# A bilinear-GLU transformer block: the order of work ahead of the first Strassen block

## The chip, the cores and the metric

The kernel runs on one core of one Trainium2 chip, in fp32. The metric is the device time of one execution in microseconds. The core has TensorE (PE, with its weight loads PEld), VectorE (DVE), ScalarE (ACT), GpSimd (POOL) and a queue for DMAs on SyncE (SP). Each engine takes its instructions in the order in which the program issues them.

## What is computed

The input x is 2048 tokens by 512. From c come six vectors: shifts, scales and gates of two adaptive layer norms.

```
h = layernorm(x) * (1 + ca) + sa
x = x + ga * (linear attention of h, 32 heads of 16) @ wo
h = layernorm(x) * (1 + cb) + sb
x = x + gb * (((h @ w_gate) * (h @ w_up)) @ w_down)      # F = 1376
```

## The kernel before

The tokens are handled in four chunks (0 to 3) of four tiles of 128. Products are made in three matmuls from a rounded high part and a low part of each operand: a split is a copy on ScalarE (L196, high part) and a subtraction (L197, low part) on VectorE or GpSimd. The schedule is manual: the order of the calls is the order on every engine.

Tiles 8 to 15 of the attention queries are flipped by VectorE: `move_in` brings a tile in block order from DRAM, `turn_v(i)` (L722) transposes its 32x32 blocks on VectorE, `turn_h(i)` (L676) makes the high part on ScalarE and `turn_l(i)` (L680) the low part on VectorE. `y_seed(i)` (L746) writes the residual into a PSUM bank on ScalarE, `y_a(i)` (L755) adds 12 matmuls to it, and `y_b(i)` copies the sum back (L763, ScalarE) and takes its layer-norm statistics (L229, VectorE). Tiles 12 to 15 alternate between two PSUM banks, so a seed waits for the statistics of the tile two before. `y_step(i)` calls `y_a(i)`, then, if the next tile has been turned but not split, its `turn_h` and `turn_l`.

The second feed-forward product pairs chunks (0, 1) and later (2, 3) in a Strassen scheme over tiles of 128 columns of F (1376 columns make ten tiles and one of 96). Columns 8 to 10 are done in the plain way for chunks 0 and 1 (`gate_up`, `down`), and `down(1, (2, 3))` is the last such call: its matmuls go out at once, and it returns a function that evacuates its two tiles, added to x, on VectorE (L824).

A Strassen block has a left and a right side. The left, `first`, is two objects `Left` (k = 0, 1); each has sums s1 to s4, and `split` makes their high and low parts on ScalarE and VectorE. The right, `rights[n]`, has four differences of 128x256 each, made by `right_sums(n, on)` (L994), and `right_split(n)`: first four high parts on ScalarE (`high`: L1005 for b11, L1008 for t1 and t2 together, t3 and t4, b21 and b22), then four low parts on GpSimd (`lows`, L1012), in that order.

`ffn()` is a generator of blocks; `fill(n)` runs n of its steps. Each block has seven products of six matmuls (`times`, L1026) in four PSUM banks a, b, c, d, in this order, with the copies on ScalarE (`copy`, L1031) between them:

```
times(a, A["a11"], R["b11"], True)
copy(b, a)
times(d, A["s1"], R["t1"], True)
copy(p5, d)
times(b, A["s2"], R["t2"], False)      # adds to the copy of a
copy(c, b); copy(u2, b)
times(a, A["a12"], R["b21"], False)
times(c, A["s3"], R["t3"], False)      # L1085 adds p5 on VectorE
times(d, A["s4"], R["b22"], False)     # L1089, L1054
times(c, A["a22"], R["t4"], False)
```

Within one product the six matmuls go by k = 0, 1, and for each k: high right with high left, high right with low left, low right with high left. At the third product VectorE also scales the down weights (L1171), and at the fifth the next block's `right_split` is issued.

In the kernel before, one `fill(1)` follows `y_step(14)`, which issues `turn_h(15)` and `turn_l(15)` behind `y_a(14)`; `turn_v(15)` stands last of VectorE's work ahead of it, behind `right_sums(0)`, the evacuations of `down(1, (2, 3))` and the low parts of s1 and s2 for k = 1.

Of the kernel before, what the change touches and what calls it, by code (L numbers as in the profile page):

```python
# [24 lines left out]
def tile_adaln_block(  # L25
# [12 lines left out]
    nc = tc.nc  # L38
# [31 lines left out]
    def f32(ap):  # L70
        return ap.bitcast(F32)
# [7 lines left out]
    def B(tag, shape=(P, D), dt=F32):  # L79

        return T(tiles, tag, shape, dt)

    def acc_bank():
        return T(ps_acc, "acc")

    def bank():
        return T(ps_w, "bank")
# [216 lines left out]
    def proj(i, w, of=bank):  # L304

        ch, j = divmod(i, NJ)
        ps = of()
        product(ps, [(cut(norm[ch].t[k], j * P, (j + 1) * P), w[k]) for k in range(KD)])
        return ps
# [43 lines left out]
    def q_a(i, ps):  # L353
        phq[i] = B("h")
        q_ps[i] = ps
        phi_a(ps, phq[i])
# [311 lines left out]
    def turn_a(i):  # L668
        tps[i] = turn_bank[0]()
        phi = phq.pop(i)  # L670
        for k in range(KD):
            nc.tensor.transpose(tps[i][:, k * P:(k + 1) * P], phi[:, k * P:(k + 1) * P], ident)

    def turn_h(i):
        pqs[i] = (B("xh", dt=F32R), B("xl", dt=F32R))
        nc.scalar.activation(pqs[i][0], tps[i], AF.Copy)  # L676

    def turn_l(i):
        h, l = pqs[i]
        nc.vector.tensor_tensor(l, tps.pop(i), f32(h), op=ALU.subtract)  # L680
# [30 lines left out]
    def move_in(*tiles):  # L711

        for i in tiles:
            v = moved[i].rearrange("(m i) (q c) -> q i m c", i=BL, c=P)
            moved[i] = B("u")
            for q in range(NQ):
                nc.sync.dma_start(moved[i][q * BL:(q + 1) * BL].rearrange("i (m c) -> i m c", c=P), v[q])

    def turn_v(i):

        tps[i] = B("f")
        nc.vector.transpose(tps[i].rearrange("p (s m i) -> p m s i", m=NQ, i=BL),  # L722
                            moved.pop(i).rearrange("p (m i s) -> p m s i", m=NQ, i=BL))

    def turned_v(i):
        turn_v(i)
        turn_h(i)
        turn_l(i)

    def ready(*tiles):  # L730
        den_c(*tiles)
        move_out(*tiles)
# [7 lines left out]
    def y_seed(i, of=acc_bank):  # L740

        yps[i] = of()
        if of is bank:

            nc.tensor.matmul(yps[i], wp[0][0][:, :P], wp[0][0], start=True, stop=True)
        nc.scalar.activation(yps[i], xts[i // NJ][i % NJ], AF.Copy)  # L746

    def y_a(i):
        if i not in yps:
            y_seed(i)  # L750
        pq = pqs.pop(i)
        for k in range(KD):
            (ah, al), (bh, bl) = cut(pq, k * P, (k + 1) * P), (wp4 if i in FLIPPED else wp)[k]
            for x, y in ((ah, bh), (ah, bl), (al, bh)):
                nc.tensor.matmul(yps[i], x, y, start=False, stop=k == KD - 1 and x is al, skip_group_check=True)  # L755

    def y_b(i):
        ch, j = divmod(i, NJ)
        ps = yps.pop(i)
        if ch in SUMS:  # L760
            norm2[ch].stats_act(j, ps)
            return
        nc.scalar.activation(xts[ch][j], ps, AF.Copy)  # L763
        norm2[ch].stats(j, of=ps)

    def y_step(i, *more, late=(), q=None, turn=True, seed=acc_bank):

        if q is not None:
            ps = proj(q, wq)
        if turn and i + 1 < NT and i + 1 not in pqs and i + 1 not in FLIPPED:  # L770
            turn_a(i + 1)
        y_a(i)
        if i + 1 in tps:
            turn_h(i + 1)
            turn_l(i + 1)
        if seed is acc_bank and i + 1 < NT:
            y_seed(i + 1, seed)
        if i - 1 in yps:
            y_b(i - 1)
        if q is not None:  # L780
            q_a(q, ps)
        if seed and i + 1 < NT and i + 1 not in yps:
            y_seed(i + 1, seed)
        for do in more:
            do()
        for do in late:
            do()
# [32 lines left out]
    def evac(ch, dn, js=range(NJ), last=False, cols=((0, D),)):  # L820
        for j in js:
            xt = xts[ch][j]
            for a, b in cols:
                nc.vector.tensor_tensor(xt[:, a:b], dn[j][:, a:b], xt[:, a:b], op=ALU.add)  # L824
                if last:
                    nc.sync.dma_start(ov[ch, j, :, a:b], xt[:, a:b])
# [26 lines left out]
    def down(ch, js=range(NJ), ahead={}, parts=(lone,), dn=None):  # L853

        dn = dn or {j: acc_bank() for j in js}
        for step, (part, j) in enumerate((part, j) for part in parts for j in js):
            for do in ahead.get(step, ()):
                do()
            a, b = j * P, (j + 1) * P
            for f in part:  # L860
                n = fts[f][1]
                (hh, hl), (dh, dl) = hs[ch, f], wf[f][2]
                nc.tensor.matmul(dn[j], hh[:n, a:b], dh[:n], start=f == lone[0], stop=False)
                nc.tensor.matmul(dn[j], hh[:n, a:b], dl[:n], start=False, stop=False)
                nc.tensor.matmul(dn[j], hl[:n, a:b], dh[:n], start=False, stop=f == lone[-1])
        return lambda: evac(ch, dn, js)
# [270 lines left out]
    def right_sums(n, on=None):  # L1137
        if n < len(steps):
            rights[n].sums(on)

    def right_split(n, on=None):
        if n < len(steps):
            rights[n].high()
            rights[n].lows(on)
# [3 lines left out]
    def draw_load(n):  # L1148
        if n < len(steps):
            f0, k = fts[steps[n][1]]  # L1150
            draws[n] = load(w_down[f0:f0 + k, :], "raw")

    banks = []
# [45 lines left out]
    def fill(n):  # L1199
        for _ in range(n):  # L1200
            next(work, None)
# [64 lines left out]
    take = down(0, ahead={1: (lambda: move_in(9), lambda: ready(11)),  # L1266
                          3: (lambda: turned_v(8), lambda: y_seed(8, bank), lambda: move_in(10, 11), lambda: turn_v(9))})
# [6 lines left out]
    first = [Left((0, 1), k).into(side) for k in range(KH)]  # L1274
# [36 lines left out]
    take = down(1, (0, 1), parts=((f0, f1), (f2,)), dn=dn, ahead={2: (lambda: y_a(12),)})  # L1311
# [1 line left out]
    take()  # L1313
    y_b(12)
    turn_v(14)
    take = down(1, (2, 3))
    first[1].sum("s1", "s3", "s2", "s4", on=nc.gpsimd)
    y_seed(14, y_bank)
    turn_h(14)
    first[0].split("s1", "s2")  # L1320
    turn_l(14)
    y_b(13)
    y_seed(15, y_bank)
    right_sums(0, nc.vector)
    take()
    first[1].split("s1", "s2")
    turn_v(15)
    for n in range(4):
        banks.append(bank())
    banks[:] = [banks[n] for n in (2, 0, 1, 3)]  # L1330
    turn_bank[0] = acc_bank
    right_split(0)
    draw_load(0)
    stash, second_side, plan = {}, {}, {}
    work = ffn()
    y_step(14, seed=None)
    fill(1)
    y_b(14)
    right_sums(1, nc.vector)
    first[0].split("s3", "s4")  # L1340
    fill(1)
    first[1].split("s3", "s4")
    fill(2)
    y_step(15)
    fill(2)
    y_b(15)
# [68 lines left out]
```

## Time and profile before

| | |
|---|---|
| Median of 3 runs | 558.47 us (558.44 to 559.93) |
| The profiled execution | 559.39 us in all, span 557.7 us |
| TensorE busy | 550.1 us, 99% of the span |
| VectorE busy | 377.8 us, 68% |
| ScalarE busy | 291.4 us, 52% |
| GpSimd busy | 203.0 us, 36% |
| Granted TensorE clock, mean | 0.997 |

A row of the timeline reads: start from the span's start, duration (of all the instructions that the row merges), engine, line, operation, output and inputs, form, count, and in brackets the idle time before it with what ended it. The start is that of dispatch; an instruction that then has to wait for a port shows a longer duration. A row of the stretches reads: from and to, then each engine's busy time with its count, the granted TensorE clock, the share of DMA and its GB/s.

### The profile page before, as it was taken

How to read it: one execution, taken by the hardware profiler on the slowest of the kernel's cores; microseconds unless marked ns; L12 is line 12 of the kernel's file. 1: busy time of each engine (PE TensorE's matmuls, PEld its weight loads, DVE VectorE, ACT ScalarE, POOL GpSimd, SP SyncE). 2: the span in 40 equal slices, each digit the busy share in tenths (PEclk: the TensorE clock that was granted, in tenths of full speed). 3: DMA queues.
4: the chain of work that ended last, by engine and by line, in shares of the span. 5: the costliest groups of instructions: out<-in, count | busy, mean ns of one | idle time of the engine just before them, and what ended most of it. 6: DMA issues, size and time to landing. Idle time of an engine off the chain costs nothing.

```text
span 557.7 us, 7356 instructions
## 1 busy us (share of the span) xinstructions
PE 550.1 (99%) x2505; PEld 451.3 (81%) x2505; DVE 377.8 (68%) x605; ACT 291.4 (52%) x539; POOL 203.0 (36%) x203
## 2 busy tenths in 40 slices
PE   8999999999999999999899999999999999999997
PEld 6888888888888878878688888887888888888886
DVE  7896968977947886877877587886553544434435
ACT  3695856646477567566683545554444444444110
POOL 2000000101012300055698666566667446446200
PEclk9899999999999999999999999999999999999999
DMA  8900203220532605846435162591335222100004
GB/s 279 384 16 2 75 25 103 101 76 1 155 100 92 188 20 169 264 143 162 132 75 148 42 201 65 188 318 29 113 114 150 59 56 58 56 21 0 1 0 150
DMA packets 59141, 60.39 MB, mean 108 GB/s; under 512 B 8608, under 2 KB 37536, under 8 KB 59104
## 3 DMA queue, kind: packets, MB, share of 16 engines
q1 hardware_dynamic: 59104, 59.93, 34.3%
q8 instruction: 19, 0.31, 0.2%
q14 instruction: 18, 0.15, 0.1%
HBM read 43.65 MB, written 16.26 MB: 107 GB/s over the span
## 4 chain that ended last, share of the span: by engine, by line
PE 92%; DVE 3%; ACT 2%; DMA 1%; issue 1%; SPq 0%; DVEq 0%; ACTq 0%
PE bank L1026 32%; PE acc L1106 6%; PE acc L1107 6%; PE acc L1108 6%; PE acc L755 5%; PE bank L209 5%; PE bank L211 5%; PE bank L210 5%; PE acc L351 3%; PE acc L349 3%; PE acc L350 3%; PE bank L839 2%; PE bank L837 2%; PE bank L838 2%; PE bank L272 2%; DMA x<-in_A_x_dram 1%
## 5 line engine op out<-in xcount | busy, mean ns | idle before, releaser
L1026 PE MATMUL bank<-h,w 128*128 128x512 f32 (+1 forms) x798 | 185.4, 390 | 1.5 <-ACT bank L1031 1.5
L1026 PEld LDWEIGHTS bank<-h,w 128*128 128x128 f32 (+1 forms) x798 | 148.1, 186 | 35.8 <-ACT bank L1031 2.6
L1031 ACT ACTIVATE bank<-bank 128x512 f32<-128x512 f32 (+1 forms) x38 | 22.1, 583 | 137.1 <-PE bank L1026 137.0
L824 DVE TENSOR_TENSOR x<-acc,x 128x512 f32<-128x512 f32 (+1 forms) x73 | 48.4, 681 | 47.4 <-PE acc L1108 47.3
L1012 POOL TENSOR_TENSOR w<-raw,w 128x256 fp32r<-128x256 f32 (+3 forms) x38 | 41.3, 1086 | 95.2 <-ACT w L1005 95.2
L1107 PE MATMUL acc<-w,kh 128*128 128x512 f32 (+2 forms) x154 | 59.6, 387 | 0.0
L1106 PE MATMUL acc<-w,kh 128*128 128x512 f32 (+2 forms) x154 | 59.6, 387 | 0.0
L1108 PE MATMUL acc<-w,kl 128*128 128x512 f32 (+2 forms) x154 | 59.5, 386 | 0.0
L197 POOL TENSOR_TENSOR w<-raw,w 128x512 fp32r<-128x512 f32 (+1 forms) x25 | 36.0, 1442 | 55.3 <-ACT w L196 28.5
L250 POOL TENSOR_TENSOR rstd<-ve,half 128x4 f32<-128x4 f32 (+1 forms) x10 | 10.8, 1080 | 120.7 <-DVE ve L249 68.0
L1012 POOL TENSOR_TENSOR w<-t,w 128x512 fp32r<-128x512 f32 (+1 forms) x38 | 49.3, 1320 | 0.0
L197 DVE TENSOR_TENSOR kl<-u,kh 128x512 fp32r<-128x512 f32 (+1 forms) x38 | 26.4, 733 | 30.2 <-ACT kh L196 30.2
L209 PE MATMUL bank<-w,h 128*128 128x512 f32 x104 | 40.8, 392 | 0.0
L211 PE MATMUL bank<-w,h 128*128 128x512 f32 x104 | 40.5, 390 | 0.0
L210 PE MATMUL bank<-w,h 128*128 128x512 f32 x104 | 40.5, 389 | 0.0
L755 PE MATMUL acc<-w,xh 128*128 128x512 f32 x120 | 37.7, 395 | 0.0
L1106 PEld LDWEIGHTS acc<-w,kh 128*128 128x128 f32 (+1 forms) x154 | 28.9, 188 | 6.0
L1108 PEld LDWEIGHTS acc<-w,kl 128*128 128x128 f32 (+1 forms) x154 | 28.9, 188 | 5.9
L1107 PEld LDWEIGHTS acc<-w,kh 128*128 128x128 f32 (+1 forms) x154 | 28.9, 188 | 5.9
L1085 DVE TENSOR_TENSOR u<-bank,u 128x512 f32<-128x512 f32 (+1 forms) x19 | 13.1, 687 | 28.9 <-PE bank L1026 22.9
L259 ACT ACTIVATE n<-x,nmr,rstd 128x512 f32<-128x512 f32 x30 | 22.9, 804 | 12.2 <-DVE nmr L254 12.2
L196 ACT ACTIVATE w<-raw 128x512 fp32r<-128x512 f32 (+2 forms) x44 | 26.3, 619 | 1.9 <-DVE raw L804 1.0
(206 smaller groups left out, 1125.1 us busy)
## 6 DMA issues: line engine op xcount, KB each, us to landing
raw<-in_w_mod_dram SPq DMA_DIRECT2D x24, 256.0 KB, 3.8
raw<-in_B_w_down_dram SPq DMA_DIRECT2D x20, 256.0 KB, 3.2
raw<-in_B_w_gate_dram SPq DMA_DIRECT2D x36, 128.0 KB, 3.7
raw<-in_B_w_up_dram SPq DMA_DIRECT2D x36, 128.0 KB, 3.6
x<-in_A_x_dram SPq DMA_DIRECT2D x16, 256.0 KB, 5.7
out_dram<-x SPq DMA_DIRECT2D x15, 256.0 KB, 2.6
raw<-in_A_wqkv_dram SPq DMA_DIRECT2D x12, 256.0 KB, 5.4
wp<-w SPq DMA_DIRECT2D x8, 256.0 KB, 3.3
```

Of the source, the lines that this page charges most:

```text
L196: nc.scalar.activation(h, src, AF.Copy)
L197: (low or nc.vector).tensor_tensor(l, src, f32(h), op=ALU.subtract)
L209: nc.tensor.matmul(ps, ah, bh, start=i == 0, stop=False)
L210: nc.tensor.matmul(ps, ah, bl, start=False, stop=False)
L211: nc.tensor.matmul(ps, al, bh, start=False, stop=i == n - 1)
L755: nc.tensor.matmul(yps[i], x, y, start=False, stop=k == KD - 1 and x is al, skip_group_check=True)
L824: nc.vector.tensor_tensor(xt[:, a:b], dn[j][:, a:b], xt[:, a:b], op=ALU.add)
L1012: sub = lambda out, x, y: (on or nc.gpsimd).tensor_tensor(out, x, f32(y), op=ALU.subtract)
L1026: mm = lambda x, y, **kw: nc.tensor.matmul(ps, x[:, k], y, skip_group_check=True, **kw)
L1106: nc.tensor.matmul(ps, hh[:, a:b], dh[:n, c:d], start=i == 0, stop=False)
L1107: nc.tensor.matmul(ps, hh[:, a:b], dl[:n, c:d], start=False, stop=False)
L1108: nc.tensor.matmul(ps, hl[:, a:b], dh[:n, c:d], start=False, stop=i == len(hs) - 1)
```

## The change

It is confined to the order of the calls ahead of and inside the first Strassen block. `turn_v(15)`, `turn_h(15)` and `turn_l(15)` are issued right behind those of tile 14 rather than around `y_step(14)`. `right_sums(0)` moves ahead of `turn_l(14)`. `right_split(0)` follows the splits of s1 and s2 for k = 0, and `right_sums(1)`, the four differences of the second right side, on VectorE, follows it, ahead of the splits of s1 and s2 for k = 1. The splits of s3 stand ahead of the first block; those of s4 stay inside it. The evacuations of `down(1, (2, 3))` go behind the block's fourth product. The four PSUM banks are no longer permuted. No instruction is added or taken away.

```
     turn_v(14)
-    take = down(1, (2, 3))
+    down_13 = down(1, (2, 3))
     first[1].sum("s1", "s3", "s2", "s4", on=nc.gpsimd)
     y_seed(14, y_bank)
     turn_h(14)
-    first[0].split("s1", "s2")
+    turn_v(15)
+    right_sums(0, nc.vector)
     turn_l(14)
+    turn_h(15)
     y_b(13)
     y_seed(15, y_bank)
-    right_sums(0, nc.vector)
-    take()
+    turn_l(15)
+    first[0].split("s1", "s2")
+    right_split(0)
+    right_sums(1, nc.vector)
     first[1].split("s1", "s2")
-    turn_v(15)
+    for x in first:
+        x.split("s3")
     for n in range(4):
         banks.append(bank())
-    banks[:] = [banks[n] for n in (2, 0, 1, 3)]
     turn_bank[0] = acc_bank
-    right_split(0)
     draw_load(0)
     stash, second_side, plan = {}, {}, {}
     work = ffn()
     y_step(14, seed=None)
     fill(1)
     y_b(14)
-    right_sums(1, nc.vector)
-    first[0].split("s3", "s4")
     fill(1)
-    first[1].split("s3", "s4")
+    for x in first:
+        x.split("s4")
     fill(2)
+    down_13()
     y_step(15)
     fill(2)
     y_b(15)
```

## The prediction

> **What bounds the kernel now.** I read the page first, then the list of TensorE's waits, then the timeline of each engine around the change, then the clock by stretches.
>
> ```profile
> span 557.7 us, 7356 instructions
> ...
> PE 550.1 (99%) x2505; PEld 451.3 (81%) x2505; DVE 377.8 (68%) x605; ACT 291.4 (52%) x539; POOL 203.0 (36%) x203
> ...
> L1026 PE MATMUL bank<-h,w 128*128 128x512 f32 (+1 forms) x798 | 185.4, 390 | 1.5 <-ACT bank L1031 1.5
> ...
> PE acc L148 <- DVE w L143: 2.0, 1, 2.0
> PE bank L1026 <- ACT bank L1031: 1.5, 1, 1.5
> PE bank L279 <- ACT n L259: 0.4, 1, 0.4
> ```
>
> TensorE is busy 550.1 of 557.7 us, and its three waits (line, releaser, total, count, longest) add up to 3.9 us. Only one of them lies where the change is: 1.5 us inside the first Strassen block. Everything after it runs with no wait, so whatever that place gains or loses arrives whole at the end, and no more than this wait and the small slips beside it can be won. The place itself, engine by engine:
>
> ```profile
> 263.59 3.19 PE L1026 MATMUL bank<-h,w 128*128 128x512 f32 x12
> 268.29 3.02 PE L1026 MATMUL bank<-h,w 128*128 128x512 f32 x12 [1.51 <-ACT bank L1031]
> 271.15 0.61 PE L755 MATMUL acc<-w,xh 128*128 128x512 f32 x2
> ...
> 273.87 23.38 PE L1026 MATMUL bank<-h,w 128*128 128x512 f32 x102
> ...
> 256.10 1.10 DVE L722 STREAM_TRANSPOSE f<-u 128x512 f32<-128x512 f32 x1
> 258.42 1.29 DVE L197 TENSOR_TENSOR h<-s,h 128x512 fp32r<-128x512 f32 x2 [1.22 <-ACT h L196]
> 259.63 0.69 DVE L680 TENSOR_TENSOR xl<-f,xh 128x512 fp32r<-128x512 f32 x1
> 260.24 0.69 DVE L229 BATCH_NORM_STATS2 st<-acc 128x6 f32<-128x512 f32 x1
> 261.06 0.39 DVE L994 TENSOR_TENSOR t<-raw 128x256 f32<-128x256 f32 x1
> ...
> 262.17 0.42 DVE L994 TENSOR_TENSOR t<-raw,t 128x256 f32<-128x256 f32 x1
> 262.50 1.28 DVE L824 TENSOR_TENSOR x<-acc,x 128x512 f32<-128x512 f32 x2
> 263.70 0.68 DVE L197 TENSOR_TENSOR h<-s,h 128x512 fp32r<-128x512 f32 x1
> 264.30 1.78 DVE L197 TENSOR_TENSOR h<-s,h 128x512 fp32r<-128x512 f32 x1
> 266.00 1.08 DVE L722 STREAM_TRANSPOSE f<-u 128x512 f32<-128x512 f32 x1
> ...
> 260.96 0.60 ACT L746 ACTIVATE acc<-x 128x512 f32<-128x512 f32 x1 [1.57 <-DVE st L229]
> 261.50 1.14 ACT L196 ACTIVATE h<-s 128x512 fp32r<-128x512 f32 x2
> 262.54 0.40 ACT L1005 ACTIVATE w<-raw 128x256 fp32r<-128x256 f32 x1
> 262.85 1.14 ACT L1008 ACTIVATE w<-t 128x512 fp32r<-128x512 f32 x2
> 263.89 0.62 ACT L1008 ACTIVATE w<-raw 128x512 fp32r<-128x512 f32 x1
> 267.12 0.63 ACT L676 ACTIVATE xh<-f 128x512 fp32r<-128x512 f32 x1 [2.61 <-DVE f L722]
> 267.66 0.58 ACT L1031 ACTIVATE bank<-bank 128x512 f32<-128x512 f32 x1
> ...
> 263.73 1.81 POOL L1012 TENSOR_TENSOR w<-t,w 128x512 fp32r<-128x512 f32 x1
> 265.50 1.73 POOL L1012 TENSOR_TENSOR w<-t,w 128x512 fp32r<-128x512 f32 x1
> 267.19 1.27 POOL L1012 TENSOR_TENSOR w<-raw,w 128x512 fp32r<-128x512 f32 x1
> ```
>
> Read it backwards. The third product of the block, at 268.29, waits for the copy L1031 at 267.66. ScalarE takes that copy only after `turn_h(15)` (L676), which had waited 2.61 us for `turn_v(15)` (L722, 266.00), last in VectorE's queue behind differences, evacuations and splits. The pace of a TensorE row is (23.38 - 0.39) / 101 = 0.227 us. The 12 matmuls from 263.59 could have ended at 266.31; the next began at 268.29. So 2.0 us is the most that a perfect order could give, 0.35%; a measurement of this kernel tells about 0.3% from no change.
>
> **What the change removes.** `turn_v(15)` follows `turn_v(14)` at once, so L676 no longer stands before the copy. Two transposes in a row take 2.05 us:
>
> ```profile
> 306.51 2.05 DVE L896 STREAM_TRANSPOSE wide<-u 128x512 f32<-128x512 f32 x2
> ```
>
> VectorE then goes: transposes 256.10 to 258.15; four differences of the first right side, 1.44 (262.50 - 261.06), to 259.6; `turn_l(14)` 0.60 (260.24 - 259.63), to 260.2, where it was before; statistics of tile 13, about 0.75, to 260.95; `turn_l(15)` to 261.6. The 16th tile costs the path nothing. ScalarE's seed L746 waits for the same statistics as before and goes at 260.9. From there ScalarE's chain is as before by its rows at 0.52 a piece: high parts of s1 and s2 for k=0 at 261.45 and 261.95, b11 at 262.5, then t12, t34 and b21/b22 until 264.35, s1 and s2 for k=1 until 265.4, two of s3 until 266.4, and the copy L1031 at 266.4 to 267.0 against 267.66 to 268.24. By that copy alone the third product could start 1.2 us sooner. The evacuations L824 (1.28 us) go behind the fourth product and read PSUM; they would fall into VectorE's wait ahead of the fifth product and cost nothing there, at most their 1.28 us without that cover. The load of the first down weights and the bank order move nothing that waits in these rows.
>
> **What it puts in the way.** The second right side's four differences now stand on VectorE ahead of the low parts of s1 and s2 for k=1, and GpSimd is at work then. The second product (`times(d, s1, t1)`) needs the low part of s1, k=1, at its fifth matmul. Before, that low part was done at 264.38. What two engines do to each other is in the rows: the VectorE subtraction dispatched at 264.30 took 1.78 instead of 0.68, ending at 266.08, 0.54 after GpSimd's row that ended at 265.54 (263.73 + 1.81); and GpSimd's next, from 265.50, ended at 267.23, 1.15 after VectorE's. They take turns, whole instruction by instruction. More of it, with a short one on GpSimd:
>
> ```profile
> 290.68 1.74 POOL L197 TENSOR_TENSOR w<-raw,w 128x512 fp32r<-128x512 f32 x1
> ...
> 291.20 1.77 DVE L197 TENSOR_TENSOR kl<-u,kh 128x512 fp32r<-128x512 f32 x1
> ...
> 292.39 1.18 POOL L994 TENSOR_TENSOR t<-raw 128x256 f32<-128x256 f32 x1
> ...
> 272.39 1.29 DVE L197 TENSOR_TENSOR h<-s,h 128x512 fp32r<-128x512 f32 x2
> ...
> 273.18 1.70 POOL L1012 TENSOR_TENSOR w<-raw,w 128x256 fp32r<-128x256 f32 x1 [4.73 <-ACT w L1005]
> ```
>
> A 256-wide GpSimd one ends at 293.57, 0.60 after VectorE's end at 292.97. No row has a 256-wide difference on VectorE against GpSimd (L994 ran there with GpSimd idle), so its price is bounded: unblocked 0.39; in turns, 0.54 - (0.68 - 0.39) = 0.25 of its own after a GpSimd instruction of 1.15. I take the turns, since each 512-wide neighbour shows them. The last two rows show that a newcomer on GpSimd can lose its first turn (1.70 for a short one while VectorE finished its subtraction and one more).
>
> The ladder: low parts of s1, s2 for k=0 at 262.1 and 262.7 to 263.3; first difference to 263.65; GpSimd's b11 low 0.60 to 264.25; second difference to 264.5; t12 low to 265.65; third to 265.9; t34 low to 267.05; fourth to 267.3; b21/b22 low to 268.45; s1 low, k=1, +0.54 to 269.0. TensorE reaches the fifth matmul of the second product at about 266.2 and waits until 269.05. Two matmuls and twelve of the third and fourth products follow: 14 x 0.227 = 3.18, and 0.14 for the restart, as at 268.29 (12 x 0.227 = 2.72 of the 2.86 until 271.15). `y_a(15)` starts at 272.4 instead of 271.15: **1.2 us later**. Queued behind the differences are also the low parts of s2, 0.6 after s1's, of s3, and the statistics of tile 14; all are in time, since s3 is first used after `y_a(15)`. GpSimd is free at 268.45 as before, and the later right sides, statistics and flips start from TensorE's products, so they shift with it.
>
> On the neighbouring fact the Trainium skill, "SBUF — State Buffer", section "Who interferes with whom", says that a VectorE instruction with two SBUF inputs contends with a GpSimd one that reads SBUF, as an exclusive lock for the whole instruction, and makes no exception for short ones. By it the sum is +1.2; by the unblocked 0.39 it would be a gain of at most 2.0.
>
> The working is against the profiled execution, 557.7 span and 559.39 in all; the median of the runs is 558.47, 0.92 lower, and I add the shift to the median: 558.47 + 1.2 = 559.7, own range 559.2 to 560.3.
>
> **Rivals.** *The clock drops (slower).* The new gap of 2.8 us (266.2 to 269.05) may cost more than itself.
>
> ```profile
> 14.00:16.00 2.00, 2.00 (x15) 1.61 (x14) 1.57 (x7) 1.24 (x3) 0.00 (x0) 0.93 1.05 386
> 16.00:18.00 2.00, 2.00 (x6) 1.60 (x5) 1.32 (x3) 2.00 (x4) 0.00 (x0) 0.50 1.05 388
> 18.00:20.00 2.00, 2.00 (x8) 1.62 (x7) 1.95 (x4) 2.00 (x4) 0.00 (x0) 0.72 1.04 385
> ...
> 266.00:268.00 2.00, 0.78 (x4) 0.30 (x2) 1.30 (x3) 0.88 (x2) 2.00 (x2) 1.00 0.00 0
> ```
>
> After the thin work ahead of 15.7 the clock (third column from the end) was 0.50 for some 3.4 us; the present gap left it at 1.00. The early drop cost 2 x (0.07 + 0.50 + 0.28) = 1.7 us of TensorE time. If the longer gap triggers it, 558.47 + 1.2 + 1.7 = 561.4. For it: the gap nearly doubles. Against it: it does not fill 3.4 us. The Trainium skill, "TensorE: Matmul & The Clock Gate", Part 1, gives a free-running window of about 3.4 us that must be idle, and would keep the clock up here or drop it by chance of the phase; the row at 16.00 shows a drop with TensorE never fully idle.
>
> *The differences aren't blocked (not slower).* With VectorE running all four in 1.44, s1's low part is there by 265.3 to 266.6. If GpSimd doesn't suffer either, the gain is 1.5 to 2.0; if it is held back for all four, b11's low part comes at 265.3 and t12's at 267.0, and the third product starts at about 268.0, a gain of 0.3. Middle: 557.4. For it: no row shows a short difference blocked. It decides from a low part of s1, k=1, ahead of 267.8.
>
> *The change trades one stall for an equal one (it doesn't do what it says).* If GpSimd loses two of its turns, as the 1.70 row shows for one, the low part comes at about 267.5: 558.5.
>
> **How the numbers follow.** Turns, clock held: 0.40. Clock drops: 0.30. Not blocked: 0.17. Equal trade: 0.10. Something else that is late: 0.03. Slower by over 0.3% (1.7 us): the clock's 0.30, the remainder 0.03, and 0.04 of the likeliest, 0.37. Faster by over 0.3%: the upper end of "not blocked", 0.05. Within: 0.58. The range from 557.3 to 561.7 takes in the middle of the gain and the clock's drop.
>
> **What would show it.** Right: VectorE's four L994 near 263.3 to 267.3 with 1 us and more between them, alternating with L1012 on GpSimd; TensorE's L1026 wait put down to VectorE's L197, 2.5 to 3 us, and the wait for L1031 gone; L676 for tile 15 near 258.3. Clock: 0.50 in the stretch behind the gap. Wrong: the four L994 back to back within 1.5 us, or L1026 without a wait over 1.5 us.

## The result and the profile after

Over 11 runs the changed kernel took 561.96 us (560.22 to 564.92) against 558.86 (558.44 to 561.85) for the kernel before: ratio 1.0053, 95% interval 1.0034 to 1.0072. It is slower by 3.1 us. The profiled execution, the slowest of the 11, took 564.92 us; its span is 563.2 and its mean granted clock 0.991. Three single runs of 610 to 929 us (of the kernel before, of "two turns less" and of "flip alone" below), at a granted clock of 0.56 to 0.85, are left out of all ratios.

TensorE's waits in the profile after (line, releaser, total, count, longest):

```profile
PE bank L1026 <- DVE h L197: 3.0, 1, 3.0
PE acc L148 <- DVE w L143: 2.0, 1, 2.0
PE bank L279 <- ACT n L259: 0.9, 1, 0.9
```

The wait for the copy L1031 is gone; a wait for VectorE's low part has taken its place, twice as long. The timeline after, by engine (start, duration, engine, line):

```profile
261.82 0.62 PE L755 MATMUL acc<-w,xh 128*128 128x512 f32 x2
...
264.55 2.58 PE L1026 MATMUL bank<-h,w 128*128 128x512 f32 x10
270.10 6.34 PE L1026 MATMUL bank<-h,w 128*128 128x512 f32 x14 [2.97 <-DVE h L197]
276.24 0.67 PE L755 MATMUL acc<-w,xh 128*128 128x512 f32 x2
...
257.06 2.08 DVE L722 STREAM_TRANSPOSE f<-u 128x512 f32<-128x512 f32 x2
...
263.01 1.29 DVE L197 TENSOR_TENSOR h<-s,h 128x512 fp32r<-128x512 f32 x2 [0.43 <-ACT h L196]
264.22 0.97 DVE L994 TENSOR_TENSOR t<-raw 128x256 f32<-128x256 f32 x1
265.22 1.41 DVE L994 TENSOR_TENSOR t<-raw,t 128x256 f32<-128x256 f32 x1
266.54 1.50 DVE L994 TENSOR_TENSOR t<-raw,raw 128x256 f32<-128x256 f32 x1
267.96 1.48 DVE L994 TENSOR_TENSOR t<-raw,t 128x256 f32<-128x256 f32 x1
269.36 2.48 DVE L197 TENSOR_TENSOR h<-s,h 128x512 fp32r<-128x512 f32 x4
...
267.35 0.57 ACT L1031 ACTIVATE bank<-bank 128x512 f32<-128x512 f32 x1
...
263.88 1.02 POOL L1012 TENSOR_TENSOR w<-raw,w 128x256 fp32r<-128x256 f32 x1 [6.30 <-ACT w L1005]
264.86 2.89 POOL L1012 TENSOR_TENSOR w<-t,w 128x512 fp32r<-128x512 f32 x2
267.72 1.44 POOL L1012 TENSOR_TENSOR w<-raw,w 128x512 fp32r<-128x512 f32 x1
```

This execution reached `y_a(14)` 0.96 us later than the profile before (261.82 against 260.86), for reasons ahead of the change, so places are best read from there. The four differences L994 took 0.97 to 1.50 us each where they had taken 0.39 to 0.43 with GpSimd idle. Each ends 0.28 us after a GpSimd instruction has ended (the first at 265.18, after b11's low part at 264.90). The low part of s1, k=1, is the first of the four from 269.36, and TensorE goes on at 270.10, 8.28 us after `y_a(14)`.

Then the clock. The stretches (from and to, busy of PE, PEld, DVE, ACT, POOL; third column from the end is the granted TensorE clock):

```profile
266.00:268.00 2.00, 1.13 (x5) 0.48 (x3) 2.00 (x3) 2.00 (x5) 2.00 (x3) 1.00 0.04 9
268.00:270.00 2.00, 0.00 (x0) 0.00 (x0) 2.00 (x4) 0.44 (x1) 1.16 (x1) 0.87 0.00 0
270.00:272.00 2.00, 1.90 (x5) 1.53 (x6) 2.00 (x5) 0.64 (x2) 0.00 (x0) 0.50 0.41 101
272.00:274.00 2.00, 2.00 (x6) 1.63 (x5) 1.97 (x5) 1.07 (x3) 0.00 (x0) 0.50 0.96 303
274.00:276.00 2.00, 2.00 (x6) 1.54 (x6) 1.67 (x3) 1.01 (x2) 0.00 (x0) 0.50 0.75 236
276.00:278.00 2.00, 2.00 (x10) 1.60 (x9) 0.00 (x0) 1.53 (x4) 0.55 (x1) 0.92 0.05 17
```

The clock fell in the gap and stayed at 0.50 past 276, 2 x (0.13 + 0.50 + 0.50 + 0.50 + 0.08) = 3.4 us of TensorE time. Both profiles also have the early drop of 3.4 us (from 15.7 before, from 16.9 here); the 0.991 counts that one too. Of the 5.5 us between the two spans, 0.96 lie ahead of the place, 4.13 between `y_a(14)` and `y_a(15)` (14.41 against 10.28), and 0.45 behind.

### The profile page after: what moved, and what is told of

Read it like the earlier page. It is cut to its first block, busy times and chain, and to the rows that moved or that the text cites. A ratio compares the mean times of both kernels' runs of the same rounds, so it can differ in the third digit from the quotient of the medians.

```text
span 563.2 us, 7359 instructions
## 1 busy us (share of the span) xinstructions
PE 553.6 (98%) x2505; PEld 453.9 (81%) x2505; DVE 380.1 (67%) x605; ACT 291.6 (52%) x539; POOL 201.9 (36%) x203
## 4 chain that ended last, share of the span: by engine, by line
PE 92%; DMA 3%; ACT 2%; DVE 2%; issue 1%; SPq 0%; ACTq 0%
PE bank L1026 30%; PE acc L755 6%; PE acc L1106 6%; PE acc L1107 6%; PE acc L1108 6%; PE bank L209 5%; PE bank L211 5%; PE bank L210 5%; PE acc L351 3%; PE acc L350 3%; PE acc L349 3%; PE bank L839 2%; PE bank L837 2%; PE bank L838 2%; PE bank L272 2%; DMA raw<-in_w_mod_dram 1%
## 5 line engine op out<-in xcount | busy, mean ns | idle before, releaser
L1026 PE MATMUL bank<-h,w 128*128 128x512 f32 (+1 forms) x798 | 188.3, 395 | 3.1 <-DVE h L197 3.0
L1026 PEld LDWEIGHTS bank<-h,w 128*128 128x128 f32 (+1 forms) x798 | 150.0, 189 | 38.2 <-DVE h L197 3.4
L1031 ACT ACTIVATE bank<-bank 128x512 f32<-128x512 f32 (+1 forms) x38 | 22.1, 582 | 139.1 <-PE bank L1026 139.1
L1085 DVE TENSOR_TENSOR u<-bank,u 128x512 f32<-128x512 f32 (+1 forms) x19 | 13.1, 689 | 32.4 <-PE bank L1026 25.6
```

The lines of the kernel that those rows point to most:

```text
L1026: mm = lambda x, y, **kw: nc.tensor.matmul(ps, x[:, k], y, skip_group_check=True, **kw)
```

## The experiments

The theory: the four differences take turns with GpSimd's four low parts, so the low part that TensorE needs comes late, and the gap that this makes lowers the clock. The rival: something else in the change (evacuations behind, bank order, early flip) costs the time, and the clock does no harm. In each kernel's trace I read three things: the time from the first matmul of `y_a(14)` to that of `y_a(15)`, TensorE's wait for L1085 behind it, and the time from `y_a(15)` to the last matmul.

| kernel | y_a(14) to y_a(15) | wait for L1085 in the first block | y_a(15) to the last matmul | time over before, runs of the same series (interval) |
|---|---|---|---|---|
| before | 10.28 | none | 282.66 | 1 |
| after | 14.41 | none | 283.11 | 1.0053 (1.0034 to 1.0072) |
| fillers in the gap | 11.68 | none | 283.07 | 1.0028 (1.0016 to 1.0039) |
| two turns less | 9.44 | none | 282.71 | 0.9983 (0.9971 to 0.9994) |
| differences behind the splits | 9.04 | 2.75 | 286.75 | 1.0066 (1.0047 to 1.0086) |
| s3 and differences behind the first product | 8.91 | 2.7 | 287.00 | 1.0065 (1.0043 to 1.0087) |
| differences and evacuations behind | 9.03 | 1.55 | 286.66 | 1.0039 (1.0023 to 1.0055) |
| all three | 9.06 | none | 283.19 | 0.9984 (0.9974 to 0.9994) |
| flip alone | 8.67 | 1.13 | 284.01 | 0.9994 (0.9982 to 1.0006) |
| flip, next split later | 8.69 | none | 282.95 | 0.9985 (0.9973 to 0.9998) |
| before with fillers | 10.28 | none | 282.67 | 1.0002 (0.9992 to 1.0013) |

**Fillers in the gap.**

```
         times(d, A["s1"], R["t1"], True)     # first block only
+        # between k = 0 and k = 1: 12 x matmul(c, b11 high, a11 high)
```

> The kernel after, with 12 more matmuls, whose result nobody reads, on TensorE between the third and the fourth matmul of the second product: 2.7 us of work in the place of the wait. Theory (of the 3 us lost, 1.2 are the late low part and the rest a drop of the clock that the gap brings on): the low part of s1 is as late as in the kernel after, the clock stays at 1.00, 1.2 us slower than before, 559.7 to 560.1, and the spread of the runs shrinks. Rival (the clock drop does no harm or is not due to the gap; the extra comes from waits behind the gap): 561.9 as the kernel after. Rival 2 (the fillers are in the way): 1 to 2 us slower than the kernel after.

Measured 560.66, ratio 1.0028. The low part is about as late as in the kernel after (the fifth matmul of the second product 8.34 us after `y_a(14)`, against 8.28), but the clock there no longer falls:

```profile
269.93 3.51 PE L1028 MATMUL bank<-h,w 128*128 128x512 f32 x14 [0.27 <-DVE h L197]
...
264.00:270.00 6.00, 5.73 (x26) 4.10 (x24) 5.96 (x7) 4.23 (x9) 4.99 (x4) 1.00 0.19 51
270.00:276.00 6.00, 6.00 (x27) 4.92 (x27) 5.46 (x10) 5.17 (x11) 1.54 (x2) 1.00 0.66 208
```

The mean clock of its 12 runs was 0.996 to 1.000. Of the 11 runs of the kernel after, two had 1.000 (spans 558.5), four 0.996 or 0.997 (559.7 to 560.2), three 0.994 (561.4 or 561.5) and two 0.991 (562.2, 563.2). The profiled run of the fillers, at 0.996, has one drop in the kernel's body, from 16.7 to 20.1 us, far ahead of the gap, so runs at 0.996 need not have dropped at the gap. The clock's part is thus shown: filling the gap, with the low part as late as ever, takes back about half of the loss. How much it is remains rough, since the two intervals (1.0034 to 1.0072 and 1.0016 to 1.0039) overlap a little. The rest, 1.8 us by the spans at a clock of 0.999 or more (558.3 to 559.0, against 556.5 to 557.6 in the runs of before beside them), is the late low part, 1.4 us, and 0.4 behind.

**Two turns less.**

```
-    right_split(0)
+    rights[0].high()
+    rights[0].lows(parts=slice(0, 1))                          # b11, t1/t2 on GpSimd
     right_sums(1, nc.vector)
     first[1].split("s1", "s2")
+    rights[0].lows(nc.vector, first=False, parts=slice(1, 3))  # t3/t4, b21/b22
```

> The kernel after, with the low parts of t3, t4 and of b21, b22 of the first right side on VectorE behind the low parts of s1 and s2 for k=1, so that GpSimd has two instructions there instead of four. Theory (the differences take turns with whole GpSimd instructions of 1.15 us): two turns less, the low part of s1 2.2 to 2.3 us sooner, about 6.0 us after the start of y_a(14) instead of 8.2, TensorE's wait 0.6 to 0.8 us instead of 3.0, no clock drop; 0.5 to 1.0 us faster than before, 557.5 to 558. Rival (the four differences cost only their own time of 1.5 us on VectorE, GpSimd does not matter): the low part as late as in the kernel after and the time 561 to 562.

Measured 557.80, ratio 0.9983. The differences' rows on VectorE, and the wait on TensorE:

```profile
263.71 0.96 DVE L994 TENSOR_TENSOR t<-raw 128x256 f32<-128x256 f32 x1
264.71 1.41 DVE L994 TENSOR_TENSOR t<-raw,t 128x256 f32<-128x256 f32 x1
266.04 0.41 DVE L994 TENSOR_TENSOR t<-raw,raw 128x256 f32<-128x256 f32 x1
266.38 0.41 DVE L994 TENSOR_TENSOR t<-raw,t 128x256 f32<-128x256 f32 x1
...
267.44 3.48 PE L1027 MATMUL bank<-h,w 128*128 128x512 f32 x14 [0.82 <-DVE h L197]
```

The first two differences still take a turn each; the last two run in 0.41. TensorE goes on 6.13 us after `y_a(14)` instead of 8.28. With the same differences in the same place on VectorE, taking two GpSimd instructions away took the loss away: the theory stands, and the rival that the differences cost only their own time falls. The evacuations, the bank order, the early flip and the early splits of s3 stand here as in the kernel after, so none of them is what made that kernel slow.

**Differences behind the splits**, then the same with s3 and the differences behind the first product and its copy.

```
-    right_sums(1, nc.vector)
     first[1].split("s1", "s2")
     for x in first:
         x.split("s3")
+    right_sums(1, nc.vector)
```

> The kernel after, with the second right side's four differences moved behind the low parts of s1 and s2 for k=1 and of s3. Theory (port turns between the differences and GpSimd's low parts, then a clock drop): the low part of s1, k=1, waits for one GpSimd instruction at most and comes about 4.8 us after the start of y_a(14) instead of 8.2; TensorE's wait of 3.0 us in the second product is gone, the clock stays at 1.00 there, the third product is set by the copy of the first bank at 6.2 us; 1.2 us faster than before, about 557.3. Rival (the time is lost by the evacuations behind the fourth product, the bank order or the early flip, not by where the differences stand): still 2 to 3 us slower than before, 561 to 562.

> The kernel after, with the splits of s3 and then the second right side's differences behind the first product and its copy. Theory: the copy of the first bank no longer stands behind s3's high parts on ScalarE and comes 1.0 us sooner, at 5.2 us after the start of y_a(14); the wait in the second product is gone, the third product starts with at most 0.1 us of wait; 1.8 to 2.0 us faster than before, about 556.6. If the copy does not matter: as with the differences behind the splits alone, 557.3. If what was lost is due to the evacuations or the bank order: 2 to 3 us slower than before.

Measured 562.74 and 562.43: the forecasts failed, although their first half held. `y_a(15)` came 1.24 and 1.37 us sooner than before. But a new wait opened in front of the seventh product, and in the first of the two it is most of the 4.1 us more from `y_a(15)` to the last matmul. The clock adds to it: one of the first kernel's six runs, at a clock of 1.000, took 561.06, the other five, at 0.993 to 0.997, 562.38 to 563.90. Rows of the same kernel:

```profile
277.70 21.21 PE L1026 MATMUL bank<-h,w 128*128 128x512 f32 x90 [2.75 <-DVE u L1085]
...
270.81 3.35 DVE L197 TENSOR_TENSOR h<-s,h 128x512 fp32r<-128x512 f32 x2
274.09 1.76 DVE L1171 TENSOR_TENSOR raw<-raw,row 128x512 f32<-128x512 f32 x1
275.77 1.28 DVE L824 TENSOR_TENSOR x<-acc,x 128x512 f32<-128x512 f32 x2
276.97 0.68 DVE L1085 TENSOR_TENSOR u<-bank,u 128x512 f32<-128x512 f32 x1
...
270.62 2.99 POOL L1012 TENSOR_TENSOR w<-t,w 128x512 fp32r<-128x512 f32 x2
273.58 1.72 POOL L1012 TENSOR_TENSOR w<-raw,w 128x512 fp32r<-128x512 f32 x1
```

When TensorE is early, ScalarE is early with the next right side's high parts, and GpSimd begins its low parts while VectorE still has s4's low parts and the scaling to do. They take turns again, and the evacuations stand behind them, in front of the addition that the seventh product waits for. In the kernel after none of this is seen, because VectorE had 4.95 us to spare there:

```profile
280.61 0.69 DVE L1085 TENSOR_TENSOR u<-bank,u 128x512 f32<-128x512 f32 x1 [4.95 <-PE bank L1026]
```

**Differences and evacuations behind.** The first of these two kernels with `down_13()` behind the second `fill(2)`.

> The kernel with the differences behind the splits, and the evacuations of down(1, (2, 3)) behind the sixth product instead of the fourth. Theory (in that kernel the addition L1085 came 2.75 us late because s4's low parts and the scaling took turns with GpSimd's next low parts, and because the two evacuations, 1.28 us, stood in front of it): the wait for L1085 shrinks by 1.2 to 1.3 us to about 1.5 us, the time at an undisturbed clock by as much, and the median by that and by a rarer clock drop: 559.5 to 561 instead of 562.7. Rival (L1085 is held by GpSimd alone, the evacuations fill a gap): wait 2.7 us, 562.7.

Measured 561.12; the wait for L1085 is 1.55 instead of 2.75, 1.2 less, about what the evacuations take. So the evacuations cost their whole time once the stage is short; that GpSimd's turns are the rest is argued here from the rows above. The time from `y_a(15)` to the last matmul is nearly the same all the same (286.66 against 286.75), because in this profile the clock fell behind the shorter wait:

```profile
276.00:278.00 2.00, 1.14 (x3) 0.97 (x4) 1.90 (x4) 1.12 (x2) 0.93 (x1) 0.79 0.81 231
278.00:280.00 2.00, 2.00 (x6) 1.55 (x5) 2.00 (x3) 0.00 (x0) 0.35 (x1) 0.50 0.56 162
```

In the profile of the kernel with the differences behind the splits, the longer wait of 2.75 us had left it at 1.00.

**All three.** The kernel with two turns less, the differences behind the splits of s1, s2 and s3, and the evacuations behind the second `fill(2)`.

> The kernel after with three edits: two low parts of the first right side on VectorE (two turns less), the second right side's differences behind the splits of s1, s2 and s3, the evacuations behind the sixth product. Theory: no wait in the second product, the third set by the copy at 6.2 us after the start of y_a(14), y_a(15) 1.2 us sooner than before; L1085 at most 0.3 us late; 1.0 to 1.3 us faster than before, 557.2 to 557.7. Rival (VectorE has too much to do before L1085 whatever the order): a wait for L1085 of 1 to 2 us, 558.5 to 560.

Measured 558.02, ratio 0.9984. In the first block it goes as expected (no wait for L1085, `y_a(15)` 1.22 us sooner), but 0.53 us are given back behind, so it gains 0.8 us by the medians (558.79 to 558.02) and not 1.0 to 1.3.

**Flip alone.** The kernel before with one part of the change.

```
     turn_h(14)
+    turn_v(15)
     first[0].split("s1", "s2")
     turn_l(14)
+    turn_h(15)
     y_b(13)
     y_seed(15, y_bank)
+    turn_l(15)
     right_sums(0, nc.vector)
     take()
     first[1].split("s1", "s2")
-    turn_v(15)
```

> The kernel before with one part of the change alone: the flip of tile 15 (turn_v, turn_h, turn_l) issued right behind that of tile 14; differences, evacuations and s3 stay. Theory (the copy of the first bank was late only because ScalarE waited for that flip; what loses in the whole change is the differences ahead of the low parts): the low part of s1, k=1, comes 4.7 us after the start of y_a(14), the third product starts 5.5 us after it instead of 7.4, y_a(15) starts 1.5 to 2.0 us sooner; a wait of 0.3 to 0.5 us for L1085 may follow; 1.2 to 1.9 us faster than before, 556.9 to 557.5. Rival (whatever is won here is given back in front of L1085, as with the differences behind the splits): a wait of 2 to 3 us for L1085, 559.5 to 561.

Measured 558.53, ratio 0.9994, which cannot be told from 1. `y_a(15)` is 1.61 us sooner, so the early flip does what it says, and 1.35 of it are lost behind, by a wait for L1085 of 1.13. Both sides were part right.

**Flip, and the next split later.** The same, with the first block's `right_split(m + 1)` behind the split of the down weights.

> The kernel before with the flip of tile 15 early (as in the run with the flip alone), and in the first block the next right side's right_split issued behind the scaling and split of the down weights instead of at the fifth product. Theory (the flip's gain of 1.6 us was given back because GpSimd's next low parts, started sooner, took turns with VectorE's low parts of s3, s4 and the scaling in front of L1085): GpSimd's four low parts start about 14 us after the start of y_a(14) instead of 9.9, VectorE's L1171 ends 12 to 12.5 us after it, no wait for L1085, y_a(15) still 1.6 us sooner; 1.3 to 1.7 us faster than before, 557.0 to 557.4. Rival (VectorE's own work is too long in front of L1085): wait of 1 us for L1085 remains, 558.5.

```profile
PE acc L148 <- DVE w L143: 2.0, 1, 2.0
...
268.90 2.50 DVE L197 TENSOR_TENSOR h<-s,h 128x512 fp32r<-128x512 f32 x4
271.31 0.69 DVE L1171 TENSOR_TENSOR raw<-raw,row 128x512 f32<-128x512 f32 x1
272.99 0.69 DVE L1085 TENSOR_TENSOR u<-bank,u 128x512 f32<-128x512 f32 x1 [0.99 <-PE bank L1026]
```

The first line is now TensorE's whole list of waits. VectorE's scaling takes 0.69 and L1085 waits for TensorE, not the other way round. Measured 558.10, ratio 0.9985: 0.5 us by the medians, where 1.3 to 1.7 were expected. In the profile 0.29 of the flip's 1.59 us are given back behind `y_a(15)`. At a clock of 1.000 its spans are 555.3 to 555.8 (4 runs), those of before 556.3 to 557.1. But 7 of its 11 runs had a clock of 0.995 or 0.996, against 7 of 21 of before at 0.997 or under. In its profile the clock stayed at 1.00 in the first block, so where it fell in those runs was not seen. This version, "two turns less" and "all three" are faster than the kernel before by 0.15%, 0.17% and 0.16%, with intervals that leave out 1.

**Before with fillers.** Seven unused matmuls in the gap of the kernel before, ahead of the third product.

> The kernel before with 7 matmuls, whose result nobody reads, ahead of the third product: 1.6 us of work in the place of its wait. Theory (a gap of 1.7 us is mostly too short to lower the clock): the same time as before within 0.1%, 558.5 to 558.9; the few runs at a clock of 0.994 become fewer. Rival (before's gap costs clock too in most runs): 1 us or more faster, 557.5.

Measured 558.79, ratio 1.0002. So the gap of the kernel before costs it no clock that can be measured, and the gap of the kernel after does.

## Why the prediction was wrong

The direction was right, and so was the mechanism of the turns; that the clock would hold was not. 559.7 was forecast, 557.3 to 561.7 was the range, and 561.96 was measured.

- *The copy of the first bank.* Forecast 266.4 to 267.0 by the old profile's times; the row starts at 267.35, which is 266.4 once the 0.96 of the later start is taken off. Right.
- *The ladder of turns.* Forecast for the low part of s1, k=1, 269.0; it ended at about 270.04 (269.36 + 0.68), which is 269.1 once the 0.96 is taken off. GpSimd took the first turn, where I had given it to VectorE; the end is the same. So a 256-wide difference on VectorE does wait for a whole GpSimd instruction, the bound I had chosen, and the 0.39 to 0.43 unblocked was the wrong one. The rule of the Trainium skill, "SBUF — State Buffer", "Who interferes with whom", which makes no exception for short instructions, agrees with the rows of L994 (0.97 to 1.50 us). The case of an equal trade put two turns at 1.5 us (269.0 to 267.5); with two turns less TensorE went on 2.15 us sooner (8.28 to 6.13).
- *The shift of `y_a(15)`.* Forecast 1.2; with fillers, at a full clock, 1.40. Under-sized by 0.2, the fillers' own hindrance not told apart.
- *"The later right sides shift with it."* Wrong by 0.4: 24.9 us behind `y_a(15)` TensorE slips once more by about 0.3 us, its weight loads waiting for L1085. The flip shows such a slip in the first block, from VectorE and GpSimd taking turns in front of that addition; what made this later one late was not traced. I had looked for what is late next only in the first block.
- *The evacuations at no cost.* Right in the kernel after, where the stall covers them; 1.2 us without that cover, as the prediction's 1.28 said.
- *The clock drop.* This is the step that failed: I let the clock hold in the likeliest case and gave a drop 0.30, because the gap does not fill 3.4 us. It need not. The Trainium skill, "TensorE: Matmul & The Clock Gate", Part 1, asks for an idle window of about 3.4 us. The rows from 266 to 270, with 1.13 us of matmuls in them, led to 0.50, and the measurement decides. The prediction's own row at 16.00, a drop with TensorE never fully idle, had pointed that way. In the runs, 9 of 11 had a mean clock of 0.997 or under, against 4 of 12 with the gap filled. An early drop ahead of 20 us may be among these; the five runs at 0.991 or 0.994 lost more than one drop of 3.4 us takes (0.003 of the mean clock, or 1.7 us).
- *The price of the drop.* 1.7 forecast. The median run, 561.96, lies 1.7 above the two runs at a clock of 1.000 (560.22 and 560.24), so as a typical price it was about right, though a mean clock does not tell where a run's drop was. In the profiled run, the slowest, the drop at the gap lasted 6.8 us, not 3.4, a price of 3.4. The rival's sum, 561.4, with the 0.2 and the 0.4 of the two points above, makes 562.0. That this meets the measured 561.96 is partly luck: its base of 558.47 was the median of three runs, and 11 runs gave 558.86.
- *The likeliest case* (turns, clock held) is the two runs at 1.000, spans 558.5 against 556.3 to 557.6 for before at that clock.

## What to carry to other kernels

When VectorE and GpSimd both work on two SBUF operands, price a short VectorE instruction at one whole GpSimd instruction for as long as GpSimd has more of them queued, and count the turns in front of what TensorE waits for. A TensorE gap of 3 us can cost as much again by the clock: 3.4 us in the profile here, and the median run lies 1.7 us above the runs at a full clock. A stall removed early in a chain brings forward the next engine's work too, and it may collide there: here 1.3 of the flip's 1.6 us stayed in the profile, and 0.5 us by the medians, only when GpSimd's next work was held back as well.

## What the runs showed that I had not expected

The gap of 3 us lowered the clock for 6.8 us in the profiled execution, though matmuls ran from 270.10 on. The gap of 1.5 us in the kernel before cost no measurable clock: fillers in it changed the time by 0.02%, interval -0.08% to 0.13%. But a wait of 1.55 us was followed by a drop in the profile of "differences and evacuations behind", and one of 2.75 us was not in that of "differences behind the splits".

The traces offer a reason. In the profile after, drops start at 16.89, 269.48 and, behind the last matmul, 563.03 us: 74 and 86 times 3.413 us apart. So the clock looks as if it were judged over fixed stretches of that length. In the stretch that ends at 269.48 TensorE was busy for 1.06 us, in the one that ends at the drop of "differences and evacuations behind" (277.15) for 1.52. Counted back in the same way from its drop at 559.24, behind its last matmul, the profile of "differences behind the splits" has its gap cut in two, and the stretches were busy for 2.10 and 1.64 us: no drop. The gap of the kernel before left 1.9 us, and no drop either. By these few stretches, what counts is how much TensorE works in one of them, so that where a gap falls matters as well as its length. No run tested this by moving a gap, and the early drop does not fit it as it stands: the stretch that ends at 16.89 shows TensorE busy for 3.11 us.
